# One bank of attention scores in eight exponentiated on VectorE, with dense projections and 17-row score matmuls

## Chip, cores and metric

One core of one Trainium2 chip. The metric is the device time of one execution in microseconds (us), as the median of several executions. Most executions of one kernel agree within a per cent or so (the four of the kernel before, taken with the changed one, lie between 1084.06 and 1095.08 us); some fall into a slower state, in which the record shows a lower granted clock of TensorE. Ratios and verdicts use the executions in the fast state alone.

## The reference

A gated sum of an attention block and a SwiGLU block over the same input, S = 2048 tokens, D = 512, 32 heads of 16, F = 1792:

```python
x = A_x
g = _sigmoid((x * gate_w).sum(-1, keepdims=True))
a = _A_ref(x, A_wqkv, A_wo)      # softmax(q k^T / 4) v, 32 heads of 16, then @ wo
b = _B_ref(x, B_w_gate, B_w_up, B_w_down)   # (silu(x wg) * (x wu)) @ wd
return g * a + (1 - g) * b
```

The attention has 32 x 2048 x 2048 = 134 million scores, each of which needs an exponential. With 128 partitions that is 1,048,576 elements on each. This is what the kernel is built around.

## The kernel before

The kernel works in 512 *slots*. A slot is one tile of 128 keys of a group of four heads, for a block of 512 queries: four banks of scores, 128 x 512 each. Four heads sit in 128 partitions, 32 apart, although a head has only 16 values: row 0 carries a bound for the softmax, rows 1 to 16 the head, rows 17 to 31 are zero, because the projection weights are padded with zeros to that layout. Scores are computed two banks at a time (two heads, each a matmul over 32 rows), exponentiated by ScalarE in one instruction of 1024 elements, and multiplied by V two slots later.

```python
    LAG = 2
    etp = ctx.enter_context(tc.tile_pool(name="etp", bufs=8))
    ps_s = ctx.enter_context(tc.tile_pool(name="ps_s", bufs=2, space=bass.MemoryType.PSUM))
    ps_o = ctx.enter_context(tc.tile_pool(name="ps_o", bufs=2, space=bass.MemoryType.PSUM))
    ps_m = ctx.enter_context(tc.tile_pool(name="ps_m", bufs=2, space=bass.MemoryType.PSUM))
    # ... (cut: loads, padded weights wkpad and wqpad, K, V, Q, bounds, gate, FFN)
    def score_pair(n, u):
        qb, g, kt = n // (G * KT), (n // KT) % G, n % KT
        qa = get_qaug(qb)
        s_t = ps_s.tile([P, 2 * QBW], F32, tag="s", name="s_t")
        for i in range(2):
            j = 2 * u + i
            mm(
                s_t[:, i * QBW:(i + 1) * QBW],
                lhsT=kaug[32 * j:32 * j + 32, g, kt * P:(kt + 1) * P],
                rhs=qa[32 * j:32 * j + 32, g, :],
                start=True, stop=True, tile_position=(32 * j, 0),
            )
        e_t = etp.tile([P, 2 * QBW], BF16, tag="e", name="e_t")
        nc.scalar.activation(out=e_t[:], in_=s_t[:], func=ACT.Exp, scale=inv_sqrt_dh)
        return e_t
    # ... (cut: attention times V, normalisation, output projection; pacing of the fillers)
    for n in range(SLOTS + LAG):
        # ... (cut: forced chains)
        if n < SLOTS:
            es[n] = [score_pair(n, 0)]
        m = n - LAG
        if m >= 0:
            pv(m, es.pop(m))
        pace.emit(n, 0.5)          # full 128 x 128 matmuls of Q, K, V, FFN, projection
        if n < SLOTS:
            es[n].append(score_pair(n, 1))
        # ... (cut)
        pace.emit(n, 0.0)
```

All matmuls run in program order. The *full* matmuls (128 x 128 weights, 512 columns) of the projections and of the SwiGLU block are fillers, doled out between the attention's matmuls.

Of the kernel before, what the change touches and what calls it, by code (L numbers as in the profile page):

```python
# [9 lines left out]
ALU = mybir.AluOpType  # L10
# [3 lines left out]
U16 = mybir.dt.uint16  # L14

# [75 lines left out]
def kernel(  # L91
# [19 lines left out]
    G = H // 4  # L111
    DC = D // P
# [9 lines left out]
    LAG = 2  # L122
    UNITS = QB * G
    SLOTS = UNITS * KT

# [3 lines left out]
    onpool = ctx.enter_context(tc.tile_pool(name="onpool", bufs=2))  # L129
    work = ctx.enter_context(tc.tile_pool(name="work", bufs=2))  # L130
    etp = ctx.enter_context(tc.tile_pool(name="etp", bufs=8))
    ffnw = ctx.enter_context(tc.tile_pool(name="ffnw", bufs=3))
    opool = ctx.enter_context(tc.tile_pool(name="opool", bufs=3))
    dram = ctx.enter_context(tc.tile_pool(name="dram", bufs=2, space=bass.MemoryType.DRAM))
    ps_s = ctx.enter_context(tc.tile_pool(name="ps_s", bufs=2, space=bass.MemoryType.PSUM))
    ps_o = ctx.enter_context(tc.tile_pool(name="ps_o", bufs=2, space=bass.MemoryType.PSUM))
# [3 lines left out]
    last_mm = [None]  # L140

    def mm(*args, **kw):
        i = nc.tensor.matmul(*args, **kw).ins  # L143
        if last_mm[0] is not None:
            tc.add_manual_dep(
                i, last_mm[0].name,
                mybir.DependencyInfo(mybir.DependencyClass.NoSync, mybir.DependencyReason.DATA),
                reason="order",
            )
        last_mm[0] = i  # L150
# [3 lines left out]
    for dc in range(DC):  # L154
        nc.sync.dma_start_transpose(out=xT[:, dc, :], in_=x[:, dc * P:(dc + 1) * P])  # L155
    mt = big.tile([P, FC, QBW], BF16, name="mt")
    wqk_raw = mt[:, :, :].rearrange("p a b -> p (a b)")[:, 0:DC * 2 * D].rearrange(
        "p (dc c) -> p dc c", dc=DC
    )
    nc.scalar.dma_start(out=wqk_raw, in_=A_wqkv[:, 0:2 * D].rearrange("(dc p) c -> p dc c", p=P))  # L160
    wv_raw = big.tile([P, DC, D], BF16, name="wv_raw")
    nc.scalar.dma_start(out=wv_raw[:], in_=A_wqkv[:, 2 * D:3 * D].rearrange("(dc p) c -> p dc c", p=P))
    gw_col = const.tile([P, DC], BF16, name="gw_col")
    nc.scalar.dma_start(out=gw_col[:], in_=gate_w.rearrange("(dc p) -> p dc", p=P))
    wd_t = big.tile([P, FC, D], BF16, name="wd_t")
    nc.scalar.dma_start(out=wd_t[:], in_=B_w_down.rearrange("(fc p) d -> p fc d", p=P))

    onescol = const.tile([P, 1], F32, name="onescol")
    nc.vector.memset(onescol[:], 0.0)
    for j in range(4):  # L170
        nc.vector.memset(onescol[32 * j:32 * j + 1, :], 1.0)

    bsel128 = const.tile([P, P], BF16, name="bsel128")
    nc.vector.memset(bsel128[:], 0.0)
    for j in range(4):
        nc.vector.memset(bsel128[32 * j:32 * j + 32, 32 * j:32 * j + 1], -1.0)
    bsel32 = const.tile([P, G, 4 * G], BF16, name="bsel32")
    nc.vector.memset(bsel32[:], 0.0)
    for g in range(G):
        for j in range(4):  # L180
            nc.vector.memset(bsel32[32 * j:32 * j + 32, g, 4 * g + j:4 * g + j + 1], -1.0)
# [4 lines left out]

    wkpad = big.tile([P, G, D], BF16, name="wkpad")
    wqpad = big.tile([P, G, D], BF16, name="wqpad")
    nc.gpsimd.memset(wkpad[:], 0.0)
    nc.gpsimd.memset(wqpad[:], 0.0)  # L190

    def padv(t, g):
        return t[:, g, :].rearrange("p (dc c) -> p dc c", dc=DC)

    def build_pad(t, col0, g):
        dst = padv(t, g).rearrange("p dc (j c) -> p dc j c", c=32)[:, :, :, 1:1 + DH]
        src = wqk_raw[:, :, col0 + g * 64:col0 + (g + 1) * 64].rearrange("p dc (j c) -> p dc j c", c=DH)
        nc.vector.tensor_copy(out=dst, in_=src)

    kaug = big.tile([P, G, S], BF16, name="kaug")  # L200
    vaug = big.tile([P, KT, G * 4 * VC + 16], BF16, name="vaug")
    nc.gpsimd.memset(vaug[:, :, G * 4 * VC:], 0.0)
    nc.gpsimd.memset(
        vaug[:, :, 0:G * 4 * VC].rearrange("p t (h c) -> p t h c", c=VC)[:, :, :, 0:1], 1.0)
    kb = const.tile([P, G], F32, name="kb")
    kneg128 = const.tile([P, G, P], BF16, name="kneg128")
    kneg32 = const.tile([P, G, 4 * G], BF16, name="kneg32")
# [4 lines left out]
    rb = big.tile([P, G, QBW], BF16, name="rb")  # L212
    acc = big.tile([P, TQ, D], F32, name="acc")

    build_pad(wkpad, D, 0)
    build_pad(wqpad, 0, 0)
    for g in range(1, G):
        build_pad(wkpad, D, g)
    for g in range(1, G):
        build_pad(wqpad, 0, g)  # L220


    def k_pieces(g, tb, act_evac=False):
        st = {}

        def pc(h):
            def f():
                if h == 0:
                    st["p"] = ps_m.tile([P, QBW], F32, tag="m", name="kp")
                for dc in (2 * h, 2 * h + 1):  # L230
                    mm(
                        st["p"][:, :], lhsT=padv(wkpad, g)[:, dc, :], rhs=xT[:, dc, tb * QBW:(tb + 1) * QBW],
                        start=(dc == 0), stop=(dc == DC - 1),
                    )
                if h == 1:
                    kseg = kaug[:, g, tb * QBW:(tb + 1) * QBW]
                    if act_evac:
                        nc.scalar.activation(out=kseg, in_=st["p"][:, :], func=ACT.Identity,  # L238
                                             bias=onescol[:, 0:1], scale=1.0)
                    else:  # L240
                        nc.vector.tensor_scalar(out=kseg, in0=st["p"][:, :], scalar1=onescol[:, 0:1],  # L241
                                                scalar2=None, op0=ALU.add)
            return f
        return [(2, pc(0)), (2, pc(1))]

    def k_bound(g, parts=1):
        w = S // parts
        if parts == 1:
            nc.vector.tensor_reduce(out=kb[:, g:g + 1], in_=kaug[:, g, :], axis=AX.X, op=ALU.max, apply_absolute_value=True)
        else:  # L250
            kp_ = work.tile([P, parts], F32, tag="kpart", name="kpart")
            for i in range(parts):
                nc.vector.tensor_reduce(out=kp_[:, i:i + 1], in_=kaug[:, g, i * w:(i + 1) * w],
                                        axis=AX.X, op=ALU.max, apply_absolute_value=True)
            nc.vector.tensor_reduce(out=kb[:, g:g + 1], in_=kp_[:, :], axis=AX.X, op=ALU.max)
        nc.vector.tensor_scalar(out=kneg128[:, g, :], in0=bsel128[:], scalar1=kb[:, g:g + 1],
                                scalar2=None, op0=ALU.mult)
        nc.vector.tensor_scalar(out=kneg32[:, g, :], in0=bsel32[:, g, :], scalar1=kb[:, g:g + 1],
                                scalar2=None, op0=ALU.mult)

    def v_pieces(tt):
        st = {}

        def pc(h):
            def f():
                if h == 0:
                    st["p"] = ps_m.tile([P, QBW], F32, tag="m", name="vp")
                for dc in (2 * h, 2 * h + 1):
                    mm(
                        st["p"][:, 0:D], lhsT=xT[:, dc, tt * P:(tt + 1) * P], rhs=wv_raw[:, dc, :],  # L270
                        start=(dc == 0), stop=(dc == DC - 1),
                    )
                if h == 1:
                    dst = vaug[:, tt, 0:G * 4 * VC].rearrange("p (h c) -> p h c", c=VC)[:, :, 1:1 + DH]
                    nc.vector.tensor_copy(out=dst, in_=st["p"][:, 0:D].rearrange("p (h c) -> p h c", c=DH))
# [3 lines left out]
    qaugs = {}  # L279

# [5 lines left out]
    def q_pieces(qb, g):  # L286
        st = {}

        def pc(h):
            def f():  # L290
                if h == 0:
                    st["p"] = ps_m.tile([P, QBW], F32, tag="m", name="qp")
                for dc in (2 * h, 2 * h + 1):
                    mm(
                        st["p"][:, :], lhsT=padv(wqpad, g)[:, dc, :], rhs=xT[:, dc, qb * QBW:(qb + 1) * QBW],
                        start=(dc == 0), stop=(dc == DC - 1),
                    )
                if h == 1:
                    nc.vector.tensor_copy(out=get_qaug(qb)[:, g, :], in_=st["p"][:, :])  # L299
# [3 lines left out]
    def abs_q(qb, g):  # L303
        aq = work.tile([P, QBW], BF16, tag="aq", name="aq")
        nc.vector.tensor_scalar(out=aq[:, :].bitcast(U16), in0=get_qaug(qb)[:, g, :].bitcast(U16),
                                scalar1=0x7FFF, scalar2=None, op0=ALU.bitwise_and)
        return aq

    def bound_one(g):
        def f():  # L310
            aq = abs_q(0, g)
            bp = ps_m.tile([P, QBW], F32, tag="m", name="bp")
            mm(bp[:, :], lhsT=kneg128[:, g, :], rhs=aq[:, :], start=True, stop=True)
            qa = get_qaug(0)[:, g, :]
            nc.vector.tensor_add(qa, qa, bp[:, :])
        return [(1, f)]

    def bound_all(qb):
        st = {}

        def pc(i):
            def f():
                if i == 0:
                    st["p"] = ps_m.tile([P, QBW], F32, tag="m", name="bpa")
                for g in (2 * i, 2 * i + 1):
                    aq = abs_q(qb, g)
                    mm(st["p"][0:4 * G, :], lhsT=kneg32[:, g, :], rhs=aq[:, :],
                                     start=(g == 0), stop=(g == G - 1))
# [326 lines left out]
```

## Time and profile before

| | before |
|---|---|
| median of 3 runs | 1090.87 us (1084.06 to 1095.00) |
| profiled run | span 1096.5 us, mean clock 0.892 |
| ScalarE / TensorE / VectorE busy | 90% / 82% / 23% |
| exponentials of 1024 elements | 1024 |
| last-ending chain, ScalarE / TensorE | 47% / 27% |

The prediction below shows the lines of the page, the windows and the timeline; they are not repeated. To read them: a row of digits cuts the span into 40 slices, and a digit is a tenth busy; the row PEclk is the clock granted to TensorE, in tenths of full speed. The clock record of the profiled run has only two values, 1 and 0.5, in its 40 entries, so the mean clock tells how long it was half: span x 2 x (1 - mean clock). The chain of waits that ended last, by engine:

```profile
ACT 47%; PE 27%; issue 17%; SPq 6%; DMA 2%; DVE 1%; another core or an unknown queue 0%; ACTq 0%; DVEq 0%
```

ScalarE carries the largest part: nearly half the span passes in its exponentials.

### The profile page before, as it was taken

The page shows a single profiled execution, that of the slowest core. Times are in us where ns is not written, and L with a number is a line of the kernel's source. Part 1 is how long each engine was busy: PE and PEld are TensorE (multiplying, and loading weights), DVE is VectorE, ACT ScalarE, POOL GpSimd, SP SyncE. Part 2 cuts the span into 40 slices and gives each one's busy share as a digit, 9 for nine tenths or more (in the row PEclk, how much of TensorE's full clock was granted, in tenths as well). Part 3 has the DMA queues.
Part 4 walks back from the last instruction along what each step waited for, and adds up shares of the span by engine and source line. Part 5 has one row for each costly group of instructions (what it writes and reads, how often), then busy time and mean ns, then how long its engine had stood idle before and what let it go on. Part 6 is the DMA issues. An engine that isn't in the chain of part 4 may idle for free.

```text
span 1096.5 us, 13996 instructions
## 1 busy us (share of the span) xinstructions
PE 902.5 (82%) x5215; PEld 228.0 (21%) x5313; DVE 247.1 (23%) x439; ACT 985.2 (90%) x1087; POOL 13.8 (1%) x14
## 2 busy tenths in 40 slices
PE   2898888988788888888888888888887888888866
PEld 0222222222112222222222222222211211121111
DVE  4443433132122111222111112221122111100013
ACT  0589999899789999999999999999987998998945
POOL 3000000010000000000000000000000000000000
PEclk9899998699869999999999989989978876897658
DMA  9000000011221000111110011110011111000010
GB/s 230 1 1 1 1 1 1 11 30 21 54 54 31 1 11 25 35 29 30 25 43 10 21 25 32 32 30 15 2 29 53 30 30 25 6 1 1 1 37 19
DMA packets 84635, 28.26 MB, mean 26 GB/s; under 512 B 75100, under 2 KB 84056, under 8 KB 84568
## 3 DMA queue, kind: packets, MB, share of 16 engines
q1 hardware_dynamic: 81176, 23.97, 9.2%
q10 hardware_dynamic: 3392, 3.41, 1.0%
q8 instruction: 41, 0.67, 0.3%
q14 instruction: 26, 0.21, 0.1%
HBM read 22.80 MB, written 2.35 MB: 23 GB/s over the span
## 4 chain that ended last, share of the span: by engine, by line
ACT 47%; PE 27%; issue 17%; SPq 6%; DMA 2%; DVE 1%; another core or an unknown queue 0%; ACTq 0%; DVEq 0%
ACT e_t L423 45%; PE s_t L143 10%; PE o_ps L143 5%; ACT th L381 2%; SPq L471 2%; PE gp L143 2%; PE kp L143 2%; SPq L335 2%; PE up L143 2%; PE vp L143 2%; PE dps L143 2%; SPq L155 2%; PE a_ps L143 1%; PE qp L143 1%; DMA xT<-in_A_x_dram 0%
## 5 line engine op out<-in xcount | busy, mean ns | idle before, releaser
L423 ACT ACTIVATE e_t<-s_t 128x1024 bf16<-128x1024 f32 x1024 | 960.0, 1031 | 72.7 <-PE s_t L143 66.9
L143 PE MATMUL s_t<-qaug,kaug 32*128 32x512 bf16 x2048 | 414.4, 417 | 134.9 <-ACT e_t L423 121.6
L143 PE MATMUL o_ps<-e_t,vaug 128*32 128x512 bf16 x2048 | 224.6, 428 | 0.7 <-ACT e_t L423 0.7
L143 PEld LDWEIGHTS <-kaug 32*128 32x128 bf16 x2048 | 101.2, 92 | 525.4 <-issue 520.0
L383 DVE SCALAR_TENSOR_TENSOR gs<-th,gp 128x512 bf16<-128x512 bf16 x56 | 38.5, 687 | 201.3 <-ACT th L381 201.3
L143 PEld LDWEIGHTS <-vaug 128*32 128x32 bf16 x2048 | 53.6, 94 | 134.8 <-issue 134.8
L143 PE MATMUL gp<-xT,wg 128*128 128x512 bf16 x202 | 73.2, 440 | 6.9 <-DMA wg<-in_B_w_gate_dram 5.1
L143 PE MATMUL up<-xT,wu 128*128 128x512 bf16 x203 | 73.0, 439 | 1.4 <-issue 1.4
L143 PE MATMUL dps<-wd_t,mt 128*128 128x512 bf16 x205 | 66.3, 402 | 2.6 <-issue 2.6
L387 DVE SCALAR_TENSOR_TENSOR mt<-gs,up 128x512 bf16<-128x512 bf16 x56 | 38.5, 687 | 119.8 <-PE up L143 110.6
L143 PE MATMUL kp<-xT,wkpad 128*128 128x512 bf16 x118 | 41.1, 434 | 22.1 <-DMA xT<-in_A_x_dram 20.6
L143 PE MATMUL a_ps<-wkpad,on_qb 128*128 128x512 bf16 x115 | 40.2, 420 | 13.6 <-DVE on_qb L474 12.6
L404 DVE TENSOR_SCALAR bblk<-dps,omg 128x512 bf16<-128x512 f32 x16 | 12.0, 750 | 146.6 <-PE dps L143 146.6
L453 DVE CAST on_qb<-o_ps 128x512 bf16<-128x512 f32 x32 | 22.1, 690 | 84.9 <-PE o_ps L143 84.9
L143 PE MATMUL qp<-xT,wqpad 128*128 128x512 bf16 x115 | 38.7, 415 | 0.8 <-issue 0.8
L241 DVE TENSOR_SCALAR kaug<-kp,onescol 128x512 bf16<-128x512 f32 x30 | 22.5, 750 | 71.7 <-PE kp L143 71.7
L299 DVE CAST qaug<-qp 128x512 bf16<-128x512 f32 x32 | 22.1, 690 | 60.4 <-PE qp L143 51.8
L381 ACT ACTIVATE th<-gp 128x512 bf16<-128x512 f32 x56 | 33.7, 602 | 1.6 <-PE gp L143 1.4
L482 DVE SCALAR_TENSOR_TENSOR o_t<-a_ps,gval,bblk 128x512 bf16<-128x512 f32 x12 | 9.0, 750 | 54.1 <-PE a_ps L143 47.4
L238 ACT ACTIVATE kaug<-kp,onescol 128x512 bf16<-128x512 f32 x2 | 1.4, 688 | 22.0 <-PE kp L143 22.0
L143 PEld LDWEIGHTS <-wg 128*128 128x128 bf16 x224 | 13.3, 99 | 36.0 <-issue 30.1
L143 PEld LDWEIGHTS <-wu 128*128 128x128 bf16 x224 | 13.4, 100 | 30.5 <-issue 29.8
(51 smaller groups left out, 186.3 us busy)
## 6 DMA issues: line engine op xcount, KB each, us to landing
wg<-in_B_w_gate_dram SPq DMA_DIRECT2D x56, 128.0 KB
wu<-in_B_w_up_dram SPq DMA_DIRECT2D x56, 128.0 KB
rb<-rr SPq DMA_DIRECT2D x124, 32.0 KB
out_dram<-o_t SPq DMA_DIRECT2D x16, 128.0 KB
dd<-on_qb SPq DMA_DIRECT2D x124, 1.0 KB
wd_t<-in_B_w_down_dram ACTq DMA_DIRECT2D x1, 1792.0 KB
qaug<-bq SPq DMA_DIRECT2D x96, 1.0 KB
mt<-in_A_wqkv_dram ACTq DMA_DIRECT2D x1, 1024.0 KB
```

What stands on the lines that cost most here:

```text
L143: i = nc.tensor.matmul(*args, **kw).ins
L155: nc.sync.dma_start_transpose(out=xT[:, dc, :], in_=x[:, dc * P:(dc + 1) * P])
L241: nc.vector.tensor_scalar(out=kseg, in0=st["p"][:, :], scalar1=onescol[:, 0:1], scalar2=None, op0=ALU.add)
L299: nc.vector.tensor_copy(out=get_qaug(qb)[:, g, :], in_=st["p"][:, :])
L335: nc.sync.dma_start(out=qa[32 * j:32 * j + 1, g, :], in_=bq[4 * g + j:4 * g + j + 1, :])
L381: nc.scalar.activation(out=th[:], in_=ps[:, :], func=ACT.Tanh, scale=0.5)
L383: nc.vector.scalar_tensor_tensor(out=gs[:], in0=th[:], scalar=1.0, in1=ps[:, :], op0=ALU.add, op1=ALU.mult)
L387: nc.vector.scalar_tensor_tensor(out=mt[:, fc, :], in0=st["gs"][:], scalar=0.5, in1=ps[:, :], op0=ALU.mult, op1=ALU.mult)
L404: nc.vector.tensor_scalar(out=bblk[:, tq, :], in0=st["p"][:, 0:D], scalar1=omg[:, t:t + 1], scalar2=None, op0=ALU.mult)
L423: nc.scalar.activation(out=e_t[:], in_=s_t[:], func=ACT.Exp, scale=inv_sqrt_dh)
L453: nc.vector.tensor_copy(out=ons[qb][:, g, :], in_=o_ps[:, :])
L471: nc.sync.dma_start(out=rb[32 * j:32 * j + 32, g, :], in_=rr[h:h + 1, :].broadcast_to([32, QBW]))
```

## The change

The intent: ScalarE is the bound, VectorE is idle three quarters of the time, so two of every sixteen banks of scores go to VectorE. It computes the exponential of a bank in 16-bit fixed point (the exponent and a fraction of nine bits in one integer), corrects the fraction by a cubic in fp16, and reads the result as bf16. To make room, the projections of K, Q and of the output use dense heads (eight in 128 rows instead of four), which needs fewer full matmuls. The heads are then spread to their rows by transfers of 16 rows each. The core of the diff:

```diff
-    LAG = 2
+    LAG = 5
+    EXP_A = 512.0 * inv_sqrt_dh * math.log2(math.e)
+    EXP_B = 512.0 * 127.0
+    def on_vector(b):
+        return b % 16 in (11, 15) and b < 4 * (SLOTS - 12)
-    etp = ctx.enter_context(tc.tile_pool(name="etp", bufs=8))
+    etp = ctx.enter_context(tc.tile_pool(name="etp", bufs=12))
-    ps_o = ctx.enter_context(tc.tile_pool(name="ps_o", bufs=2, space=bass.MemoryType.PSUM))
+    ps_d = ctx.enter_context(tc.tile_pool(name="ps_d", bufs=1, space=bass.MemoryType.PSUM))
+    ps_o = ctx.enter_context(tc.tile_pool(name="ps_o", bufs=1, space=bass.MemoryType.PSUM))
 ... (cut: strict program order for ScalarE and VectorE too; dense wqk)
+    def spread_heads(t, b, src, c0, c1, first_on=None):
+        for h in range(8):
+            g, j = 2 * b + h // 4, h % 4
+            eng = nc.sync if first_on is None or h % 2 == 0 else first_on
+            eng.dma_start(out=t[32 * j + 1:32 * j + 1 + DH, g, c0:c1], in_=src[DH * h:DH * (h + 1), 0:c1 - c0])
 ... (cut)
-                lhsT=kaug[32 * j:32 * j + 32, g, kt * P:(kt + 1) * P],
-                rhs=qa[32 * j:32 * j + 32, g, :],
+        mm(ps, lhsT=kaug[32 * j:32 * j + VC, g, kt * P:(kt + 1) * P],
+           rhs=get_qaug(qb)[32 * j:32 * j + VC, g, :], start=True, stop=True, tile_position=(32 * j, 0))
 ... (cut)
+    def vec_bank(b, last):
+        d_t = ps_d.tile([P, QBW], F32, tag="d", name="d_t")
+        score(d_t[:, :], b)
 ... (cut: first step y = EXP_A * score + EXP_B into uint16; after two banks, on 1024 elements:)
+                lambda: vec.tensor_scalar(out=za, in0=ya, scalar1=0x1FF, scalar2=None, op0=ALU.bitwise_and),
+                lambda: vec.tensor_scalar(out=ua, in0=za, scalar1=EXP_C3, scalar2=EXP_C2, op0=ALU.mult, op1=ALU.add),
+                lambda: vec.tensor_tensor(out=ua, in0=ua, in1=za, op=ALU.mult),
+                lambda: vec.tensor_scalar(out=ua, in0=ua, scalar1=EXP_C1, scalar2=EXP_S, op0=ALU.add, op1=ALU.mult),
+                lambda: vec.tensor_tensor(out=ua, in0=ua, in1=za, op=ALU.mult),
+                lambda: vec.tensor_tensor(out=ya, in0=ya, in1=ua, op=ALU.add),
+                lambda: (vec.tensor_scalar(out=ya, in0=ya, scalar1=0.25, scalar2=None, op0=ALU.mult),
 ... (cut: order of banks, up to two slots of attention-times-V in a slot or none, normalisation)
```

`32 * j + 32` became `32 * j + VC`, with VC = 17: the spread by transfers never writes rows 17 to 31 of Q, so the score matmul now leaves them out. The result is the same, since those rows were zero.

## The prediction

Two terms of the VectorE sum were four one-source operations on 1024 elements (1.70 us together) and three two-source ones (2.07); with two reads of a PSUM bank (1.38) the sum came to 5.15 us a pair and 644 us in all. The trace before has these operations on 512 elements alone, so what 1024 cost was not shown. Rival (c): its "hard form" supposed that steps mixing uint16 and fp16 are slower and came to about 1190 us; the trace before has no such step.

> **What bounds the kernel now.** I read the page first (engine totals, then the span in slices), then the groups of instructions, then engine times in windows of 10 us, then the timeline of two short stretches.
>
> The totals say that ScalarE (ACT) comes first, TensorE (PE) second, and that VectorE (DVE) is idle three quarters of the time. The slices say that the middle is flat, with holes where the granted clock of TensorE is low.
>
> ```profile
> PE 902.5 (82%) x5215; PEld 228.0 (21%) x5313; DVE 247.1 (23%) x439; ACT 985.2 (90%) x1087; POOL 13.8 (1%) x14
> PE   2898888988788888888888888888887888888866
> ACT  0589999899789999999999999999987998998945
> PEclk9899998699869999999999989989978876897658
> ```
>
> The groups show what ScalarE does: 1024 exponentials over two banks of scores (128x1024). Each costs 960.0/1024 = 0.9375 us, less than the single duration of 1031 ns because neighbours overlap. Its idle time, 72.7 us, is nearly all spent waiting for TensorE's score matmuls.
>
> ```profile
> L423 ACT ACTIVATE e_t<-s_t 128x1024 bf16<-128x1024 f32 x1024 | 960.0, 1031 | 72.7 <-PE s_t L143 66.9
> L143 PE MATMUL s_t<-qaug,kaug 32*128 32x512 bf16 x2048 | 414.4, 417 | 134.9 <-ACT e_t L423 121.6
> L143 PE MATMUL o_ps<-e_t,vaug 128*32 128x512 bf16 x2048 | 224.6, 428 | 0.7 <-ACT e_t L423 0.7
> ```
>
> The windows (columns: stretch, length, busy PE, PEld, DVE, ACT, POOL, granted clock, DMA share, GB/s) separate three regimes. At full clock ACT is 100% busy. At half clock ACT falls to 84 to 87%: TensorE is the bound there. And there are a few holes, one around the last normalisation.
>
> ```profile
> 450.00:460.00 10.00, 8.40 (x53) 2.23 (x53) 2.65 (x4) 10.00 (x13) 0.00 (x0) 1.00 0.18 41
> 920.00:930.00 10.00, 9.61 (x43) 1.88 (x41) 1.37 (x2) 8.42 (x10) 0.00 (x0) 0.50 0.12 27
> 1050.00:1060.00 10.00, 2.36 (x5) 0.51 (x6) 1.70 (x4) 0.75 (x2) 0.00 (x0) 0.50 0.21 69
> ```
>
> The mean clock is 0.892. If it is either 1 or 0.5, it was half for 2 x 0.108 x 1096 = 237 us. At 14% lost, that is about 30 of the 72.7 us of idle ACT. The timeline shows a slot (one key tile of four heads) at full clock, then steps at half clock:
>
> ```profile
> 500.10 0.39 PE L143 MATMUL s_t<-qaug,kaug 32*128 32x512 bf16 x2 [0.26 <-ACT e_t L423]
> 500.42 0.40 PE L143 MATMUL o_ps<-e_t,vaug 128*32 128x512 bf16 x4
> 500.75 0.60 PE L143 MATMUL gp<-xT,wg 128*128 128x512 bf16 x2
> 501.29 0.39 PE L143 MATMUL s_t<-qaug,kaug 32*128 32x512 bf16 x2
> ...
> 1062.96 0.60 PE L143 MATMUL s_t<-qaug,kaug 32*128 32x512 bf16 x2
> 1063.49 0.62 PE L143 MATMUL o_ps<-e_t,vaug 128*32 128x512 bf16 x4
> 1065.37 1.03 PE L143 MATMUL a_ps<-wkpad,on_qb 128*128 128x512 bf16 x2
> ```
>
> From start to start at full clock: a score pair 0.32 us, the four attention-times-V matmuls 0.33, two full matmuls 0.53. At half clock: 0.53, 0.54, 0.96.
>
> [...] Arithmetic mixing uint16 and fp16 occurs nowhere in this trace[...].
> [...] The trace's clock record does step in multiples of 3.413 us between 1 and 0.5. In it half clock mostly follows windows with two or fewer full 128x128 matmuls; windows with four mostly stay at full.
>
> ```profile
> L305 DVE TENSOR_SCALAR aq<-qaug 128x512 uint16<-128x512 uint16 x32 | 8.6, 292 | 10.8 <-PE bpa L143 10.5
> L474 DVE TENSOR_TENSOR on_qb<-on_qb,rb 128x512 bf16<-128x512 bf16 x31 | 12.7, 422 | 27.5 <-DMA rb<-rr 27.5
> L453 DVE CAST on_qb<-o_ps 128x512 bf16<-128x512 f32 x32 | 22.1, 690 | 84.9 <-PE o_ps L143 84.9
> ```
>
> **The change, part by part.** I count in groups of four slots; there are 128 in the 512 slots.
>
> *ScalarE.* 250 of the 2048 banks leave (two in sixteen, except the last 12 slots), so 899 exponentials remain. 125 x 0.9375 = 117 us go; about 4 us of new copies for K, Q and V at the start come. ACT busy: 985 - 117 + 4 = 872 us. Per group: 7 x 0.9375 + 0.23 for the tanh = 6.8 us, where before it was 7.7.
>
> *VectorE.* Per pair of banks: two reads of a PSUM bank at 0.69[...]. Sum 1.38 + 1.70 + 2.07 = 5.15 us, times 125 = 644. Each of the seven depends on the one before; dependent neighbours in the old trace start 0.03 us after the end, so the pair occupies 5.4. Old work that goes: kaug 22.5, qaug 22.1 and 5.5, reductions 18.6, weight padding 6.9, absolute values 8.6, norm 12.7, bq 2, together 99; its thinner replacements come to about 50 (14 K and 15 Q copies at 0.69, 16 reductions at 0.68, half as many absolute values and products, 7 bq, memsets). Rest 247 - 99 + 50 = 198. DVE busy about 840 us; in the steady part 5.4 + 1.4 = 6.8 us a group. That is the same as ScalarE: no slack between the two.
>
> *TensorE.* Dense heads (eight in 128 rows, not four) halve the full matmuls for K, Q and the output projection: counted in program order 1152 become 944. A steady group has 7 full matmuls, not 8.6. Group at full clock: 9 score issues x 0.32 (seven pairs, two single banks) + 4 x 0.33 + 3.5 x 0.53 = 6.1 us: under 6.8, at 89%. At half clock the old kernel takes 7.7/0.86 = about 9.0 us with such fillers and 8.7 where they are thin; the new one saves 1.6 x 0.48 and pays up to 0.53 for the split pair: about 8.4.
>
> *PSUM and waits.* The score tiles keep two buffers, the vector banks get one, the attention output has one, not two. A late DVE therefore stops TensorE in order at the next vector bank, and with it ScalarE. The delay of five slots and twelve exponential tiles soften this for the V matmuls, not for that one bank.
>
> *Edges.* First exponential: 34 us before. Now K and Q heads go out by DMA: 20 issues on each of two queues; at the 0.31 to 0.53 us that one issue took before, estimated 6 us later, 40. The 28 broadcasts of the last normalisation (12.8 us of queue time, the hole above) become four: perhaps 8 us of the hole go. End after the last exponential stays 12 us.
>
> *Sum.* Between bound (6.8) and coupling I take 7.1 us a group at full clock, 8.4 at half. With half clock for 22% of the time as before: 1/(0.78/7.1 + 0.22/8.4) = 7.35 us, x 128 = 941. Plus 40 + 12: 993, rounded to 992.
>
> **Rivals.**
> (a) *Clean gain.* Every group runs at ScalarE's 6.8: 870 + 52 = 922 us, plus half clock as before about 955. For it: the counts balance exactly. Against: three engines at 89 to 100% in strict order, one buffer each between them.
> (b) *The clock.* Full matmuls per slot fall from 2.16 to 1.7, about the density of the old kernel's last fifth (1.8), where about 40% of the time was at half clock. Against: slots are shorter, so density in time falls less. With 45% at half: 128 x 7.63 + 52 = 1029.
> (c) *VectorE becomes the bound.* Waits of in-order DVE for tanh or PSUM add 0.5 us a group: 7.6 at full clock, 1045. [...]
> (d) *Hidden anyway*: ScalarE gains nothing because TensorE holds it. At full clock ACT is at 100%, so I give this little.
>
> **Range and chances.** (a) gives the low end 955, (b) the high end 1035. Faster by over 2% needs less than 1069 us; only (c) in its hard form misses that. Faster 0.93, same 0.04, slower 0.03.
>
> **What would show it.** ACT busy near 872 with 899 exponentials; the seven DVE steps at 0.43 and 0.69 us, DVE busy near 840; PE waiting for DVE at the single score bank; mean clock near 0.89; first exponential near 40 us. A DVE step above 1 us, mean clock below 0.8, or long PE waits for DVE would each make the prediction wrong upwards; ACT at 100% with clock above 0.95, downwards.

Four of its statements, in numbers of the same trace. The entries of the clock record last one or several times 3.413 us; of such windows with two or fewer full matmuls 51 of 95 were followed by half clock, of those with three or four 14 of 166 (the table further down). The last fifth of the span has a mean clock of 0.74, so half clock for 52% of it, not the 40% of rival (b). At half clock ScalarE is busy 77% in the mean, not the 84 to 87% of the windows read. The 0.23 us a group for the tanh was an estimate: two exponentials with a tanh between them start 0.46 us further apart than two without, 56 times in the trace, which makes 0.20.

## The result, and the profile after

The changed kernel takes 1228.96 us (median of 4 runs, 1225.99 to 1258.53; the last of these is slow). The kernel before has 1092.93 in the same company. The ratio of fast runs is 1.1253, 95% interval 1.1166 to 1.134: 12.5% slower, where 9% faster was predicted. Ratios here and below are the mean time of one kernel's fast runs over that of the other's of the same rounds, so they are not quite the ratio of the medians quoted.

The engine totals of the profiled run:

```profile
PE 1082.0 (88%) x5109; PEld 207.3 (17%) x5109; DVE 811.8 (66%) x1475; ACT 898.9 (73%) x967; POOL 16.3 (1%) x23
```

ScalarE did lose its work: 985 us became 899. VectorE took it: 247 became 812. But TensorE, which has 204 weight loads (and so matmuls) fewer than before, 5109 instead of 5313, is busy 180 us longer. The slices say why (rows PE, ACT and the granted clock):

```profile
PE   2877899999999999989999899899888899999875
ACT  0666677777767688788767787887878678877863
PEclk9796555555565556577565675756676555555555
```

Where the clock row had nines with a few holes, it now has fives. The mean clock is 0.598, so the clock was half for about 985 of 1225 us. The chain of waits has moved from ScalarE to TensorE:

```profile
PE 64%; ACT 15%; issue 7%; DVE 7%; SPq 4%; DMA 2%; ACTq 0%; DVEq 0%
```

The groups (busy time, mean ns of one, then idle time before them and what ended it):

```profile
L172 ACT ACTIVATE e_t<-s_t 128x1024 bf16<-128x1024 f32 x899 | 866.6, 1027 | 262.4 <-PE s_t L169 256.0
L169 PE MATMUL s_t<-qaug,kaug 17*128 17x512 bf16 x1798 | 425.2, 551 | 62.5 <-ACT e_t L172 58.3
...
L178 DVE TENSOR_TENSOR u_t<-u_t,z_t 128x1024 f16<-128x1024 f16 x250 | 173.1, 692 | 8.6
...
L169 PE MATMUL d_t<-qaug,kaug 17*128 17x512 bf16 x250 | 139.3, 557 | 13.2 <-DVE y_t L178 13.1
...
L178 DVE TENSOR_SCALAR u_t<-z_t 128x1024 f16<-128x1024 uint16 x125 | 53.4, 427 | 4.3
```

The 899 exponentials cost what they should, but ScalarE waits 256 us for the score matmuls, where before it waited 67. A score matmul takes 551 ns in the mean instead of 417. VectorE's steps take 427 and 692 ns as predicted, and at the bank of the new path TensorE waits for VectorE only 13 us in all. The new path is not what is late.

Two stretches of 50 us (busy PE, PEld, DVE, ACT, POOL, granted clock, DMA share, GB/s):

```profile
150.00:200.00 50.00, 47.71 (x253) 9.70 (x253) 36.19 (x71) 38.30 (x43) 0.00 (x0) 0.50 0.09 23
500.00:550.00 50.00, 45.01 (x230) 9.00 (x229) 37.52 (x67) 41.36 (x46) 0.00 (x0) 0.69 0.13 31
```

In the first, TensorE is busy 95% of the time and the clock is half throughout. The timeline of TensorE shows the moment at which the clock falls, 502.3 us in the clock record (start, length, instruction):

```profile
500.60 0.39 PE L169 MATMUL s_t<-qaug,kaug 17*128 17x512 bf16 x2 [0.94 <-ACT e_t L172]
...
501.83 0.40 PE L169 MATMUL o_ps<-e_t,vaug 128*32 128x512 bf16 x4
502.17 0.93 PE L169 MATMUL up<-xT,wu 128*128 128x512 bf16 x2
...
503.99 0.62 PE L169 MATMUL o_ps<-e_t,vaug 128*32 128x512 bf16 x3
504.00 0.61 PE L169 MATMUL o_ps<-y_t,vaug 128*32 128x512 bf16 x1
```

The four matmuls with V overlap: one alone takes 390 ns in the mean at full clock, all four together 0.40 us, and at half clock three of them take 0.62. In the first line, at full clock, a pair of 17-row score matmuls takes 0.39 us, just as the 32-row pair does in the kernel before. Over the whole traces a score matmul takes 381 ns in the mean at full clock and 599 to 601 at half, with 17 rows as with 32; a full one, over 128 rows, takes 384 at full clock. So the thinner matmul is no slower in itself: only the clock differs.

### The profile page after: what moved, and what is told of

It reads as the page before. It is cut to its first block, busy times and chain, and to the rows that moved or that the text cites. A ratio compares the mean times of both kernels' runs of the same rounds, so it can differ in the third digit from the quotient of the medians.

```text
span 1225.0 us, 14674 instructions
## 1 busy us (share of the span) xinstructions
PE 1082.0 (88%) x5109; PEld 207.3 (17%) x5109; DVE 811.8 (66%) x1475; ACT 898.9 (73%) x967; POOL 16.3 (1%) x23
## 4 chain that ended last, share of the span: by engine, by line
PE 64%; ACT 15%; issue 7%; DVE 7%; SPq 4%; DMA 2%; ACTq 0%; DVEq 0%
PE s_t L169 15%; PE o_ps L169 15%; ACT e_t L172 14%; PE d_t L169 8%; PE dps L169 7%; PE up L169 7%; PE gp L169 6%; PE a_ps L169 2%; PE qp L169 2%; DVE u_t L178 2%; SPq L185 2%; SPq L256 2%; DVE y_t L178 2%; PE vp L169 1%; PE kp L169 1%
## 5 line engine op out<-in xcount | busy, mean ns | idle before, releaser
L172 ACT ACTIVATE e_t<-s_t 128x1024 bf16<-128x1024 f32 x899 | 866.6, 1027 | 262.4 <-PE s_t L169 256.0
L169 PE MATMUL s_t<-qaug,kaug 17*128 17x512 bf16 x1798 | 425.2, 551 | 62.5 <-ACT e_t L172 58.3
L178 DVE TENSOR_SCALAR y_t<-d_t 128x512 uint16<-128x512 f32 x250 | 172.0, 688 | 224.4 <-PE s_t L169 194.8
L169 PE MATMUL o_ps<-e_t,vaug 128*32 128x512 bf16 x1798 | 289.7, 565 | 3.3 <-ACT e_t L172 3.3
L178 DVE TENSOR_TENSOR u_t<-u_t,z_t 128x1024 f16<-128x1024 f16 x250 | 173.1, 692 | 8.6
L169 PEld LDWEIGHTS <-kaug 17*128 17x128 bf16 x2048 | 85.5, 98 | 526.4 <-issue 525.0
L169 PE MATMUL d_t<-qaug,kaug 17*128 17x512 bf16 x250 | 139.3, 557 | 13.2 <-DVE y_t L178 13.1
L169 PE MATMUL o_ps<-y_t,vaug 128*32 128x512 bf16 x250 | 141.4, 565 | 0.9 <-DVE y_t L178 0.9
L178 DVE TENSOR_TENSOR y_t<-y_t,u_t 128x1024 uint16<-128x1024 uint16 x125 | 86.5, 692 | 4.3
L178 DVE TENSOR_SCALAR u_t<-z_t 128x1024 f16<-128x1024 uint16 x125 | 53.4, 427 | 4.3
```

The lines of the kernel that those rows point to most:

```text
L169: ordered(nc.tensor.matmul(*args, **kw))
L172: ordered(nc.scalar.activation(*args, **kw))
L178: return lambda *a, **kw: ordered(f(*a, **kw))
```

## The experiments

Three guesses at why the clock fell from 0.892 to 0.598. Theory A: because the score matmuls use 17 rows, not 32. Theory B: because the dense projections took full matmuls away (944 in place of 1152 in program order). Theory C: because the coupling to VectorE makes holes in TensorE. All kernels below gave correct results.

### e1: the changed kernel with 32 rows

```diff
             qaugs[qb] = qpool.tile([P, G, QBW], BF16, tag="qaug", name="qaug")
+            nc.gpsimd.memset(qaugs[qb][:], 0.0)
-        mm(ps, lhsT=kaug[32 * j:32 * j + VC, g, kt * P:(kt + 1) * P],
-           rhs=get_qaug(qb)[32 * j:32 * j + VC, g, :], start=True, ...
+        mm(ps, lhsT=kaug[32 * j:32 * j + 32, g, kt * P:(kt + 1) * P],
+           rhs=get_qaug(qb)[32 * j:32 * j + 32, g, :], start=True, ...
```

> The changed kernel, but each score matmul contracts 32 rows of the array again (the 15 rows beyond the 17 used hold zeros), not 17. Theory A[...]: mean clock back to 0.85 or more, time 960 to 1020 us. Theory B (too few full matmuls per time): clock stays near 0.6, time near 1225. Theory C (in-order waits on VectorE and ScalarE leave TensorE idle[...]): clock near 0.6, time near 1225.

Measured: 1094.66 us (1093.79 to 1103.81), ratio to before 1.0027 (0.9973 to 1.0081), clock 0.819. The clock slices and the score group:

```profile
PEclk9898775898985699998985898889997866889655
```

```profile
L169 PE MATMUL s_t<-qaug,kaug 32*128 32x512 bf16 x1798 | 374.4, 445 | 115.0 <-ACT e_t L172 110.1
```

Fifteen more rows, all multiplied by zeros, make the kernel 134 us faster. This is nearly the whole loss. It is not a gain over the kernel before, though: the clock stays a little under the 0.85 that was expected from A and the time misses the expected 960 to 1020 us, so something else is missing too.

### e2: the kernel before with 17 rows

```diff
-                lhsT=kaug[32 * j:32 * j + 32, g, kt * P:(kt + 1) * P],
-                rhs=qa[32 * j:32 * j + 32, g, :],
+                lhsT=kaug[32 * j:32 * j + VC, g, kt * P:(kt + 1) * P],
+                rhs=qa[32 * j:32 * j + VC, g, :],
```

> The kernel before, with one edit: its score matmuls contract 17 rows, not 32 (the same result, the other rows are zero). Theory A: mean clock falls from 0.89 to 0.6-0.75, time rises to 1150-1250 us. Theories B and C: nothing changes, 1085-1100 us and clock 0.89, as neither the full matmuls nor the waits are touched.

Measured: 1265.59 us median (1236.29 to 1281.15). Three of the four runs count as slow, so there is no ratio; but the fastest, 1236.29 at a clock of 0.659, is 14% above the fastest run of before in the same rounds (1088.95, clock 0.915). The totals and the clock slices of the profiled run, which is one of the slow ones:

```profile
PE 1160.3 (91%) x5215; PEld 229.9 (18%) x5313; DVE 248.8 (19%) x439; ACT 1016.8 (79%) x1087; POOL 13.8 (1%) x14
```

```profile
PEclk9896555557676556575676555558565555555555
```

The same instructions in the same order, with neither offload nor dense projections, and the clock falls as in the changed kernel: it is half for about 1035 of 1279 us. TensorE is busy 91% of the time. Between 60 and 1195 us the trace has one stretch of 3.1 us without a matmul and no other above 0.63 us, so idleness does not explain the fall here. The kernel before, between 60 and 1040 us, has longer such stretches, of 5.1 and 2.4 us, at its higher clock. Rows 17 to 31 are zero in K and in Q here, since both come from zero weights, so the data in them do not explain it either. (Ends of matmuls are modelled in the trace, so the length of a gap is approximate.) A holds in both directions; the median is above the 1150 to 1250 us that were expected from it, the fastest run within.

### e13 and e14: 24 rows in both kernels

The edits are those of e1 and e2 with `32 * j + 24`.

> A dose test of the rows theory: the changed kernel with the score matmuls over 24 rows (the seven extra are zero in Q) between the 17 of the change (1229 us, clock 0.60) and the 32 of the first experiment (1095 us, clock 0.82). [...] the result lies clearly between: 1120 to 1190 us, clock 0.66 to 0.77. [...] If the extra rows only matter in that they are a multiple of 32, also 1229.

> The same dose in the old kernel: 24 rows between 32 (1093 us, clock 0.89) and 17 (1266 us, clock 0.60). Rows weighed: 1120 to 1200 us, clock 0.70 to 0.82. A threshold at the full group of 32 rows: about 1265 us. No dependence between 24 and 32: about 1093 us.

Measured: the changed kernel with 24 rows takes 1172.18 us (1163.47 to 1182.55), ratio 1.0795 (1.0705 to 1.0885), clock 0.708. The kernel before with 24 rows takes 1144.45 us (1143.28 to 1166.03), ratio 1.0505 (1.0447 to 1.0564), clock 0.806. One of the four executions of each is slow (1182.55 and 1166.03). The clock slices of the first and then of the second:

```profile
PEclk9795565986776687985868755676875665667555
```

```profile
PEclk9897996559599999778899577999976767576657
```

| rows of a score matmul | changed kernel, us (clock) | kernel before, us (clock) |
|---|---|---|
| 17 | 1229 (0.60) | fastest 1236 (0.66); the profiled run, slow, 1281 (0.60) |
| 24 | 1172 (0.71) | 1144 (0.81) |
| 32 | 1095 (0.82) | 1093 (0.89) |

The effect is graded: 24 rows lie between in both kernels, at a clock of 0.71 between 0.60 and 0.82, and of 0.81 between 0.66 and 0.89. A single step somewhere between 17 and 32 rows, with 24 like one of the two, is ruled out for both kernels.

### e3: more full matmuls in the changed kernel

```diff
+                if h == 0:
+                    for _ in range(2):
+                        mm(ps[:, :], lhsT=w[:, 0, :], rhs=xT[:, 0, qb * QBW:(qb + 1) * QBW], start=True, stop=True)
```

Ahead of each gate and up product, two full matmuls whose result is overwritten: 224 in all, about what the dense projections saved.

> The changed kernel with 224 full 128x128 matmuls more (two ahead of each gate and up product, overwritten by the next one), so 2.2 full ones per slot as in the kernel before. Theory B: clock back to about 0.85, time about 1050 or less although there is more work. Theory A: clock rises some, since full matmuls also count, perhaps to 0.75, time 1100-1200. Theory C: more work on the bound engine at the same half clock, time 1290-1330.

Measured: 1217.24 us (1201.87 to 1228.05), two of the four runs slow; ratio of the fast ones (1201.87 and 1210.59) 1.1028 (1.0951 to 1.1106), clock 0.702. Theory B is right that they count too: the clock rises by 0.1. But they have to be paid for, and the time falls only by about 2% (ratio 1.1028 for 1.1253). The thinner fillers cannot be the main cause.

### e4: the changed kernel without the offload

```diff
     def on_vector(b):
-        return b % 16 in (11, 15) and b < 4 * (SLOTS - 12)
+        return False
```

> The changed kernel with no bank on VectorE: all 1024 exponentials on ScalarE as before, the rest of the restructuring kept. Theory C: clock and time go back to those of before or better, 1060-1095 us, clock near 0.89. Theories A and B: the clock stays near 0.6 and TensorE keeps the time at 1200-1260 us, since the scores still contract 17 rows and the full matmuls are as few.

Measured: 1268.01 us (1259.98 to 1278.75), ratio 1.1587 (1.1491 to 1.1683), clock 0.571. Without the work on VectorE, the kernel is slower still. C falls, here and by e2, which has no coupling to VectorE at all. The offload itself helps, by 3% even where the clock is half.

### e5, e6 and e8: why 32 rows bring no gain

In e1 VectorE waits 12.4 us between 75 and 145 us for the transfers that spread K to free a staging buffer. e5 is e1 with four such buffers:

```diff
-                    kst[(b, tb)] = work.tile([P, QBW], BF16, tag="kst", name="kst")
+                    kst[(b, tb)] = work.tile([P, QBW], BF16, tag="kst", name="kst", bufs=4)
```

> The changed kernel with scores of 32 rows, and four buffers, not two, for the tile from which the K heads are spread by DMA. In the run with 32 rows alone VectorE waited 12.4 us for those DMAs between 75 and 145 us, and TensorE and ScalarE behind it. If that wait is on the path, 1070 to 1085 us, with ScalarE's wait for scores in that stretch nearly gone; if it only moves to the next DMA wait, 1090 to 1100.

Measured: 1086.26 us (1082.68 to 1090.38), ratio 0.9961 (0.9928 to 0.9994), clock 0.829: 8 us better than e1, measured in other rounds (0.7% by the ratios, whose intervals overlap a little). e6 and e8 add full matmuls to it, to lift the clock: e6 one ahead of each bank for VectorE (250), e8 the 224 of e3.

```diff
         d_t = ps_d.tile([P, QBW], F32, tag="d", name="d_t")
+        mm(d_t[:, :], lhsT=wd_t[:, 0, 0:P], rhs=xT[:, 0, 0:QBW], start=True, stop=True)
```

> As the kernel with four buffers, and one full 128x128 matmul more ahead of each single score bank (250, overwritten by the score), evenly spread, so 2.2 full ones a slot as in the kernel before. If the thinner full matmuls are the second cause of the low clock (theory B in its weaker form): clock from 0.82 to 0.92 or more, time 1000 to 1050. If the added work costs as much as the clock gives: 1070 to 1100.

> As the kernel with four buffers, and 224 full matmuls more, ahead of the gate and up products in pairs, so only where full matmuls already stand. Theory B: clock 0.88 or more, time 1010 to 1060, a little worse than the evenly spread ones, because the thin windows stay thin. Otherwise 1080 to 1110.

Measured: e6 1093.11 us (1089.59 to 1097.83), ratio 1.0024 (0.9984 to 1.0063), clock 0.886; e8 1089.20 us (1087.52 to 1091.43), ratio 0.9988 (0.9966 to 1.0009), clock 0.871. The clock is nearly back at the level of before, and the time has not fallen: the added matmuls take what the clock gives. Laid over the clock record, seven exponentials (four slots) take about 7.5 us at full clock and 11 at half in e6, where e5 takes 7.2 to 7.3 and about 10; e6 is at half clock for 250 us instead of 369. The timeline of e6 shows another kind of loss, here after one block of queries (first a line of VectorE, then one of ScalarE; in brackets the idle time before and its releaser):

```profile
335.61 0.95 DVE L178 RECIPROCAL rn<-dn 128x128 bf16<-128x128 bf16 x1 [3.83 <-DMA dn<-dd]
...
338.42 1.02 ACT L172 ACTIVATE e_t<-s_t 128x1024 bf16<-128x1024 f32 x1 [3.60 <-PE s_t L169]
```

VectorE, which now works in strict order, stands for a transfer at the reciprocal; the single bank of its path stays full, TensorE stops in order at it (2.9 us idle until VectorE has read the bank), and ScalarE runs dry for 3.6 us.

### e7 and e9: 32 rows, without the offload

e7 is e1 with `on_vector` returning False; e9 adds the 224 full matmuls of e3.

> Scores of 32 rows, and no bank on VectorE: what the offload is worth where the row count is as before. By the prediction's sum ScalarE gains 117 us: this kernel 1150 to 1200 us against 1095 with the offload. If the offload is given back to TensorE's half clock: within 2% of it, 1090 to 1115.

> Scores of 32 rows, no bank on VectorE, and 224 full matmuls more (two ahead of each gate and up product), which brings the full ones per slot back to the 2.2 of the kernel before. If the thinner full matmuls are why the kernel without the offload took 1179 us and not 1092: clock from 0.75 to about 0.88, time 1090 to 1120. If the rest of the rebuilding costs it (order, single output bank, later start): clock may rise but the time stays 1150 or more.

Measured: e7 1179.05 us (1177.65 to 1185.06), ratio 1.0821 (1.0787 to 1.0855), clock 0.753; e9 1196.99 us (1192.96 to 1202.17), ratio 1.095 (1.085 to 1.105), clock 0.803. So at 32 rows the offload is worth 1179 - 1095 = 84 us. But the kernel rebuilt for it is 86 us slower than before when the offload is taken out. The clock slices and the exponentials of e7:

```profile
PEclk9796556896788976687787779788866685788555
```

```profile
L172 ACT ACTIVATE e_t<-s_t 128x1024 bf16<-128x1024 f32 x1024 | 970.2, 1033 | 122.8 <-PE s_t L169 113.6
```

At full clock ScalarE is 98% busy in e7, as before. It is half clock that costs: 555 us of it between the first and the last exponential, against 228 before. Yet more full matmuls (e9) do not repair it: they lengthen every slot. Eight exponentials take about 10.5 us at half clock and 8.1 at full, against 9.8 to 10.0 and 7.8 in e7.

### e15: the old delay and two output banks in e7

```diff
-    LAG = 5
+    LAG = 2
-    ps_d = ctx.enter_context(tc.tile_pool(name="ps_d", bufs=1, space=bass.MemoryType.PSUM))
-    ps_o = ctx.enter_context(tc.tile_pool(name="ps_o", bufs=1, space=bass.MemoryType.PSUM))
+    ps_o = ctx.enter_context(tc.tile_pool(name="ps_o", bufs=2, space=bass.MemoryType.PSUM))
```

> What in the rebuilt kernel costs the 86 us that 32 rows without the offload (1179 us) lies above the kernel before. This run takes that kernel and gives it back the old delay of two slots and two output banks (the bank of the vector path is unused there). If the delay of five slots with its empty and double slots of attention-times-V and the single output bank are the cause: 1090 to 1120 us. If the cause is the strict order on VectorE and ScalarE, the K and Q spread by transfers or the thinner full matmuls: 1160 to 1190 us.

Measured: 1189.16 us (1182.63 to 1191.28), ratio 1.0909 (1.0848 to 1.097), clock 0.731. The longer delay and the single output bank are not what costs the 86 us. What is left of the rebuilding was not taken apart: the strict order on VectorE and ScalarE, the spread of K and Q by transfers, where the fillers fall in time, and the dense projections in ways that e9 does not undo.

### e10: the offload in the kernel before

The vector path, its order of banks, the delay of five slots and the strict order, put into the kernel before with its padded projections and 32 rows (e_t gets ten buffers, the cubic's two work tiles one each, the output tile two instead of three; reciprocal and normalising products are emitted later, much as in e11).

> The kernel before with the offload alone: its padded K, Q and output projection and its 32-row scores kept, one bank in eight to VectorE with the changed kernel's group order, delay, and single banks for that score and for the output. If the low clock was the whole fault: clock about 0.88, time 985 to 1030 us. If the in-order coupling of the engines gives the gain back at any clock: 1060 to 1100.

Measured: 1162.58 us (1157.70 to 1168.17), ratio 1.0632 (1.0548 to 1.0716), clock 0.814. The exponentials:

```profile
L166 ACT ACTIVATE e_t<-s_t 128x1024 bf16<-128x1024 f32 x899 | 861.9, 1029 | 229.6 <-PE s_t L163 181.6
```

ScalarE saves about 98 us of exponentials and waits 157 us longer. The offload without the dense projections loses. That it loses because VectorE (854 us busy here, 812 in e1) and TensorE are not relieved is argued, not shown: this version also differs in the buffers named.

### e11 and e12: a version that beats both

e11 is e5 with the reciprocal emitted four slots later and the normalising products three slots before they are needed, so that VectorE does not stand for transfers in order:

```diff
-        vops.append(spread)
+        later.append((now[0] + (4 if qb < QB - 1 else 1), spread))
-                    if tq == 0:
+                    if tq == 0 and g1 < G:
+    for qb in range(QB - 1):
+        later.append(((qb + 1) * G * KT + LAG + 11, lambda qb=qb: [norm(qb, b, P) for b in range(NB)]))
```

e12 adds the 250 full matmuls of e6.

> The kernel with 32 rows and four K buffers, with two pieces of VectorE's order moved: the reciprocal of the denominators four slots later and the normalising products three slots ahead of the projection, so that VectorE does not stand in front of a DMA while a score bank waits. The stands seen were 3.8 us and 2.4 to 4.3 us a query block: 1060 to 1075 if they are on the path, 1083 to 1090 if not.

> The same with one full matmul more ahead of each single score bank. If the stands also pulled the clock down: 1045 to 1075 and clock above 0.9. If added TensorE work costs what the clock gives, as without the moves: 1070 to 1090.

Measured: e11 1067.42 us (1066.13 to 1077.65), ratio 0.9781 (0.9697 to 0.9864), clock 0.824; e12 1070.35 us (1067.05 to 1077.32), ratio 0.9795 (0.9718 to 0.9873), clock 0.895. The reciprocals, all forms but the last block's, in e5 and then in e11:

```profile
L178 DVE RECIPROCAL rn<-dn 128x128 bf16<-128x128 bf16 x3 | 2.9, 954 | 8.7 <-DMA dn<-dd 8.7
```

```profile
L178 DVE RECIPROCAL rn<-dn 128x128 bf16<-128x128 bf16 x3 | 2.8, 944 | 0.0
```

The stand of 8.7 us is gone, TensorE's wait for normalised values ahead of the projection falls from 16.5 to 6.1 us, and the time falls by 19 us (1.8% by the ratios, in different rounds). The two moves were not run apart. e11 is the fastest kernel of the study, 2.2% under the kernel before (the interval reaches to 1.4%, so the verdict at 2% is unclear) and 13% under the changed one. Lifting the clock further with dummy matmuls again gives nothing.

## Why the prediction was wrong, point by point

**The right steps.** 899 exponentials, as counted. ScalarE busy 899 us against 872 predicted. The VectorE steps at 427 and 692 ns, against 0.43 and 0.69 us. On 1024 elements the one-source step from uint16 to fp16 took 427 ns, where uint16 to uint16 took 424 to 427 and fp16 to fp16 422; all two-source steps, of fp16 and uint16, took 692. So rival (c) in its hard form is out. VectorE busy 812 us against about 840. TensorE does wait at the single bank, but only 13 us. First exponential at 44.0 us (40 predicted), 15.1 us from the end of the last to the end of the kernel (12 predicted): the edges cost 7 us more.

**The failed step.** The sum took "With half clock for 22% of the time as before", and the passage on TensorE counted only full matmuls, in number and in time. It did not ask what the 17 rows do to the clock, although the diff shows them, and read the trace's relation between clock and full matmuls as if the score matmuls counted the same in both kernels. The runs show that they do not. e1 and e2 isolate the two lines: 134 us one way, 147 us between the fastest runs (1236.29 - 1088.95) the other. The kept traces also show it window by window. The entries of the clock record last multiples of 3.413 us; the table counts, in each such window between the first and the last exponential, the full matmuls (by their weight loads, since some matmul records are missing: 5215 for 5313 loads in the kernel before) and asks whether the next window is at half clock:

| rows, kernel | at half after 0 to 2 full matmuls | after 3 or 4 | after 5 or more |
|---|---|---|---|
| 32, before | 51 of 95 | 14 of 166 | 0 of 45 |
| 32, e1 | 98 of 159 | 12 of 128 | 0 of 18 |
| 24, e14 | 85 of 112 | 38 of 168 | 1 of 39 |
| 24, e13 | 151 of 179 | 40 of 128 | 0 of 15 |
| 17, changed | 203 of 206 | 77 of 123 | 1 of 12 |
| 17, e2 (slow run) | 167 of 169 | 129 of 173 | 2 of 18 |

So what the prediction read in the old trace was there, but it belonged to 32 rows: at the same number of full matmuls, 17 rows are followed by half clock far more often, in the old kernel as in the new. The two counts are not the whole measure: e7, with 32 rows, has 135 of 183 and 28 of 130.

Overlaying the clock record on the exponentials, the changed kernel is at half clock for 82% of the time between the first and the last of them, not 22%.

How much of the miss this is can be worked out from the same overlay. It gives for a group of four slots (7 exponentials) 7.5 us at full clock and 9.5 us at half in the changed kernel, where 7.1 and 8.4 had been predicted.

| change to the sum, 899/7 = 128.4 groups | us |
|---|---|
| as predicted | 993 |
| half clock 82% of the time instead of 22%, predicted group times: 128.4 / (0.18/7.1 + 0.82/8.4) + 52 | about 1096 |
| with the measured group times 7.5 and 9.5: 128.4 / (0.18/7.5 + 0.82/9.5) + 52 | about 1216 |
| edges of 59 us instead of 52 | about 1223 |

So the share of half clock is one mis-sized term, and the group at half clock is a second of the same weight. The 8.4 us came from two short windows in which ScalarE was 84 to 87% busy. Over all its half clock the kernel before had ScalarE only 77% busy, 10.4 us for 8 exponentials instead of 9.0, so that half clock went with about 52 us of idle ScalarE, not 30. The windows chosen were too kind. In the predicted mix of 22% this error would have been worth 22 us (9.5 for 8.4 in the sum); with 82% and the full-clock group of 7.5 the group times make 120.

**Rival (b), "the clock",** named the right bound for a wrong reason. It put 45% half clock down to fewer full matmuls and came to 1029 us. Those do count (e3: clock 0.60 to 0.70 by 224 of them), but with 32 rows the changed kernel would have been at 1095 (e1), with half clock for 36% of its span. That is no more half clock than (b) foresaw; it lands higher in time, because the group at half clock then costs 10.3 to 10.4 us, again far from the predicted 8.4.

**Rival (d), "hidden anyway",** got little weight because ScalarE was 100% busy at full clock (98% over all of the full clock in the trace before). That argument was sound only as long as the clock stayed full; yet even at half clock for most of the time the offload brought 3% (e4).

**What stays open.** What the granted clock follows. The runs show that it rises with the rows of the score matmuls and with the number of full matmuls, and that in e2 neither idle time nor data explain the fall. They give points, not a rule: in the changed kernel 224 full matmuls more lifted the mean clock from 0.60 to 0.70 (e3), seven rows more per score matmul from 0.60 to 0.71 (e13), fifteen from 0.60 to 0.82 (e1). The matmul and its weight load change their rows together in every run, so which of the two counts is not separated. And which part of the rebuilding costs the 86 us in e7: extra full matmuls (e9) and the delay and banks (e15) are excluded, the rest was not separated.

## What to carry to other kernels

When TensorE is near the bound, check the granted clock before anything else, and treat an edit of the rows of a matmul as a possible edit of the clock: trimming rows of zeros saved no time of its own here (381 ns a score matmul at full clock, before as after) and cost a tenth of the kernel (134 of 1229 us). When a prediction multiplies by a clock share, take the cost at half clock from all of the time at half clock, not from a window that looks typical. And when an engine works in strict order with one buffer to the next, emit whatever waits for a transfer late enough that it never waits.
